# Decode attention with an MLP: the w4 contraction ahead of the last values, outputs laid out by one masked product, the last chunks in two column halves

## The chip, the core and the metric

The kernel runs on one core of a Trainium2 chip. The core has a matrix engine (PE, with a separate row for its weight loads, PEld), a vector engine (DVE), a scalar engine (ACT), a general engine (POOL), a queue that issues most transfers (SP), and 16 DMA engines. Matrix products are written to PSUM, everything else lives in SBUF, and the inputs and the output are in HBM. Each engine works through its own instructions in order; engines wait for each other through semaphores.

The metric is the device time of one execution in microseconds (us), the median over several runs. One more execution is profiled; all durations in this document that are not called a median come from such a profile.

## What is computed

One decode step for 4 sequences, an attention block and an MLP side by side on the same normalized input. The cut reference:

```python
xn = layernorm(x)                                # x: (4, 1, 512)
xa = layernorm(xn)                               # the MLP's own norm; xn is what both blocks get
q  = (xn @ wq).reshape(4, 1, 32, 128).transpose(0, 2, 1, 3)
s  = einsum("bhqd,bhkd->bhqk", q, k_cache) * 128 ** -0.5
o  = einsum("bhqk,bhkd->bhqd", softmax(s), v_cache)
A  = o.transpose(0, 2, 1, 3).reshape(4, 1, 4096) @ wo
B  = xn + gelu(xa @ w3) @ w4                     # with one position, the token mixing adds nothing
out = x + A + B
```

The caches are 4 x 32 x 4096 x 128 in float32: 268 MB each for K and V. wq is 512 x 4096 and wo 4096 x 512 (8.39 MB each), w3 512 x 1792 and w4 1792 x 512 (3.67 MB each). The token mixing shifts along the sequence, which has one position, so all of its shifted parts are zero and w1 and w2 are not read. Everything is float32.

## The kernel before

**Pairs.** The 128 heads (4 sequences of 32) are taken as 64 pairs. K and V of one pair are 4.19 MB each and fill one buffer of 128 partitions x 8192 numbers; partitions 0 to 63 hold the one head, 64 to 127 the other. All large loads, w3, wq (two), K and V, w4 and wo (two), take turns in six such buffers (`slot`, L72), in the order in which the code asks for them; a load is issued by SP when the buffer that is six requests older has been read.

**One pair.** DVE multiplies K by the broadcast query in two pieces (`products`, L199) and adds up along the head dimension (`row_sums`, L203). The maximum over the positions needs a small transpose on PE (`max_begin`, L208 and L210) and a broadcast back (`weights`, L216 to L220). ACT then takes the exponentials (L228) into the blocks of a weight tile that POOL clears (L224). `values` (L238) multiplies weights and V on PE, 16 products of 32 weight columns by 512 columns; product g goes to the partitions 32t to 32t+31 of PSUM with t = g mod 4, which is one of four column groups of the array. In float32 the hardware runs each such product as two passes, so the profile counts twice as many matmuls.

**The loop** (L292 to L313) runs over i from 0 to 64. It asks for K and V of pair i+1, starts pair i on DVE and finishes pair i-1 on ACT and PE. After four pairs `outputs` (L243 to L256) takes the eight heads' results out of PSUM: a copy by ACT into `os`, four products with `sel` and one with `ones` into `oz`, a reciprocal and a product on DVE into `OT`, which has a column for each head. After the 32 heads of a sequence, `spread` (L258 to L264) lays the columns of `OT` out into `lt` with four copies on ACT, each of 32 partitions to every fourth column; the rest of `lt` is zero. One product with `sel` then gives 128 x 32, which becomes `X[:, :, b]`, the left operand for wo.

**The MLP.** `mlp_up` (L269 to L285) runs near the start and leaves gelu(xa @ w3), transposed, in `gT`.

**The end** (L316 to L361). w4 is requested after V of the last pair, wo after w4 in five pieces (chunks 0-15, 16-23, 24-27, 28-30 and 31; a chunk is 128 rows of wo). The first four left operands of w4 are 32 columns wide, zero but for 4, and are made by POOL in the free part of w4's buffer (L321, L322). On PE: `y` gets 14 products with w4 (L341) and those with chunks 0 to 23 (L344), 512 columns each, in four strips of 32 partitions whose sum is wanted. ACT copies `y` to SBUF. `total`, 128 x 128 in PSUM, holds the output's 512 columns as four strips of 128; it was given x + xn at the start (L168). It now gets chunks 24 to 27 (L350), the four strips of `y` added up by a product with `sel` (L352), and chunks 28 to 31 (L355), each as four products of 128 columns. DVE copies `total` to SBUF (L358), and four stores, two each issued by SP and ACT, write the output (L361).

The tile framework orders the instructions of an engine by its own planning and not strictly by the code: on PE one w4 product of `y` stands before `oz`, eight between `oz` and `xt`, and five behind `xt`.

Of the kernel before, what the change touches and what calls it, by code (L numbers as in the profile page):

```python
# [29 lines left out]
F32 = mybir.dt.float32  # L30
AF = mybir.ActivationFunctionType
ALU = mybir.AluOpType
AX = mybir.AxisListType
PSUM = bass.MemoryType.PSUM

P = 128
# [7 lines left out]
def decode_block(ctx: ExitStack, tc: tile.TileContext, x, k, v, wq, wo, w3, w4, out):  # L44
    nc = tc.nc
    B, H, S, DH = k.shape
    D = wq.shape[0]
    F = w3.shape[1]
    NC = D // P
    NF = F // P  # L50
# [3 lines left out]
    NP = B * H // 2  # L54
# [6 lines left out]
    consts = ctx.enter_context(tc.tile_pool(name="consts", bufs=1))  # L61
    kv = ctx.enter_context(tc.tile_pool(name="kv", bufs=SLOTS))
    work = ctx.enter_context(tc.tile_pool(name="work", bufs=2))
    psum = ctx.enter_context(tc.tile_pool(name="psum", bufs=2, space=PSUM))
# [7 lines left out]
    def slot(name):  # L72
        return kv.tile([P, R * DH], F32, tag="kv", name=name)

    def pair_rows(flat, i):
        n = 2 * S * DH
        return flat[i * n:(i + 1) * n].rearrange("(p c d) -> p c d", p=P, c=R)
# [8 lines left out]
    for h in range(2):  # L86
        t = slot(f"wq{h}").rearrange("p (c n) -> p c n", c=NC // 2)
# [5 lines left out]
    def load_k(i):  # L93
        K[i] = slot(f"k{i}").rearrange("p (c d) -> p c d", c=R)
        nc.sync.dma_start(K[i], pair_rows(kf, i))

    def load_v(i):
        V[i] = slot(f"v{i}").rearrange("p (c d) -> p c d", c=R)
        nc.sync.dma_start(V[i], pair_rows(vf, i))
# [6 lines left out]
    ident = consts.tile([P, P], F32, name="ident")  # L106
# [6 lines left out]
    sel = consts.tile([P, 32], F32, name="sel")  # L113
    nc.vector.reduce_sum(sel, ident.rearrange("p (q m) -> p m q", q=4), axis=AX.X)

    selb = consts.tile([P, B, 2, HALF], F32, name="selb")
    for e in range(2):
        a, z = (ident[:, 32 * q:32 * q + B].unsqueeze(2).to_broadcast([P, B, HALF]) for q in (e, e + 2))
# [9 lines left out]
    lt = consts.tile([P, H, 4], F32, name="lt")  # L128

    X = consts.tile([P, WC, B], F32, name="X")  # L130
# [31 lines left out]
    x1nT = lt.rearrange("p h q -> p (h q)").rearrange("p (c m) -> p c m", c=NC)  # L162
    transposed(x1n, x1nT, "x1nT")

    total = psum.tile([P, P], F32, tag="base", bufs=1, name="total")
    for t in range(4):
        for n, src in enumerate((xs, xn)):
            nc.tensor.matmul(total[32 * t:32 * t + 32, :], ident[:B, 0:32], src[:, P * t:P * t + P],  # L168
                             start=(n == 0), stop=False)
    nc.gpsimd.memset(pw_all, 0.0)  # L170
    PW = [pw_all[:, n, :].rearrange("p (g m) -> p g m", g=NG) for n in range(2)]

# [1 line left out]
    q_sb = consts.tile([P, 2, 512], F32, name="q_sb")  # L174
    pq = [psum.tile([P, 512], F32, tag="pv", name=f"pq{n}") for n in range(2)]
    for c in range(NC):
        w = wq_sb[c // 2][:, c % 2, :].rearrange("p (u n j e d) -> p u n e j d", u=2, n=2, j=4, e=2)
        for n in range(2):
            for u in range(2):
                for e in range(2):  # L180
                    r0 = 32 * (2 * u + e)
                    nc.tensor.matmul(pq[n][r0:r0 + 32, :], xnT[:, c, :], w[:, u, n, e],  # L182
                                     start=(c == 0), stop=(c == NC - 1))
# [6 lines left out]
    def queries(z):  # L190
        b, zz = divmod(z, QB)
        u, n = divmod(zz, 2)
        QBC[z] = psum.tile([P, QUAD, DH], F32, tag="qb", name=f"qb{z}")
        nc.tensor.matmul(QBC[z], selb[HALF * u:HALF * (u + 1), b], q_sb[HALF * u:HALF * (u + 1), n, :],  # L194
                         start=True, stop=True)

    def products(i, c0, c1):
        q = QBC[i // QUAD][:, i % QUAD, :].unsqueeze(1).to_broadcast([P, c1 - c0, DH])
        nc.vector.tensor_tensor(out=K[i][:, c0:c1, :], in0=K[i][:, c0:c1, :], in1=q, op=ALU.mult)  # L199

    def row_sums(i):
        sc = work.tile([P, R], F32, tag="sc", name=f"sc{i}")
        nc.vector.reduce_sum(sc, K[i], axis=AX.X)  # L203
        SC[i] = sc

    def max_begin(i):
        rm = work.tile([P, 1], F32, tag="rm", name=f"rm{i}")
        nc.vector.reduce_max(rm, SC[i], axis=AX.X)  # L208
        pm = psum.tile([1, P], F32, tag="b", name=f"pm{i}")
        nc.tensor.matmul(pm, rm, ident, start=True, stop=True)  # L210
        ROWMAX[i] = pm
# [19 lines left out]
    def values(i):  # L231
        z, r = divmod(i, QUAD)
        if r == 0:
            PVS[z] = psum.tile([P, 4 * DH], F32, tag="pv", name=f"pv{z}")
        pw, pv = PW[i % 2], PVS[z]
        for g in range(NG):
            t = g % 4
            nc.tensor.matmul(pv[32 * t:32 * t + 32, :], pw[:, g, :], V[i][:, 4 * g:4 * g + 4, :],  # L238
                             start=(r == 0 and g < 4), stop=(r == QUAD - 1 and g >= NG - 4))

    OT = {}
# [14 lines left out]
        nc.vector.tensor_mul(OT[b][:, 8 * zz:8 * zz + 8], oz[:, 0, :], rz)  # L256

    def spread(b):  # L258
        for q in range(4):
            s = slice(32 * q, 32 * q + 32)  # L260
            nc.scalar.copy(lt[s, :, q], OT[b][s, :])  # L261
        pt = psum.tile([P, 32], F32, tag="b", name=f"xt{b}")
        nc.tensor.matmul(pt, lt, sel, start=True, stop=True)  # L263
        nc.scalar.copy(X[:, :, b], pt)  # L264


    gT = consts.tile([P, NF, B], F32, name="gT")

    def mlp_up():  # L269
        ph = psum.tile([P, FT], F32, tag="qb", name="ph")  # L270
        for c in range(NC):
            for t in range(4):
                nc.tensor.matmul(ph[32 * t:32 * t + 32, :], x1nT[:, c, :],
                                 w3_sb[:, c // 2, c % 2, t * FT:(t + 1) * FT],
                                 start=(c == 0), stop=(c == NC - 1))
        hs, u, t, gt = (w3_slot[:, n * FT:(n + 1) * FT] for n in range(4))
        nc.scalar.copy(hs.rearrange("p (m i) -> p m i", i=32), ph.rearrange("p (i m) -> p m i", i=32))
        nc.vector.tensor_mul(u, hs, hs)
        nc.vector.tensor_scalar(u, u, GELU_B, 1.0, op0=ALU.mult, op1=ALU.add)
        nc.vector.tensor_mul(u, u, hs)  # L280
        nc.scalar.activation(t, u, AF.Tanh, scale=GELU_A)
        nc.vector.tensor_scalar(t, t, 1.0, 0.5, op0=ALU.add, op1=ALU.mult)
        nc.vector.tensor_mul(hs, hs, t)
        nc.vector.transpose(gt, hs)
        nc.vector.tensor_copy(gT, gt.rearrange("p (m i) -> p m i", i=32)[:, :, 0:B])  # L285


    load_v(0)
    queries(0)
    mlp_up()  # L290
    nc.gpsimd.memset(lt, 0.0)
    for i in range(NP + 1):  # L292
        if i + 1 < NP:
            load_k(i + 1)
            load_v(i + 1)
        if i < NP:
            if i % QUAD == 0 and i // QUAD + 1 < NQ:
                queries(i // QUAD + 1)
            products(i, 0, 16)
        if i > 0:  # L300
            weights(i - 1)
        if i < NP:
            products(i, 16, R)
            row_sums(i)
        if i > 0:
            values(i - 1)
            if i % QUAD == 0:
                z = i // QUAD - 1
                outputs(z)
                if z % QB == QB - 1:  # L310
                    spread(z // QB)
        if i < NP:
            max_begin(i)  # L313


    w4_slot = slot("w4")  # L316
    w4_sb = w4_slot[:, :NF * D].rearrange("p (m n) -> p m n", m=NF)
    w4_r = w4.rearrange("(p m) n -> p m n", m=NF)
    nc.sync.dma_start(w4_sb, w4_r)
    gT0 = w4_slot[:, NF * D:NF * D + 4 * 32].rearrange("p (m i) -> p m i", m=4)  # L320
    nc.gpsimd.memset(gT0, 0.0)  # L321
    nc.gpsimd.tensor_copy(gT0[:, :, 0:B], gT[:, 0:4, :])  # L322
    wo_r = wo.rearrange("(p c) n -> p c n", c=WC)
    wo_sb = [slot(f"wo{n}").rearrange("p (c n) -> p c n", c=WC // 2) for n in range(2)]

# [5 lines left out]
    for c0, c1 in ((0, 16), (16, CUT), (CUT, 28), (28, 31), (31, WC)):  # L331
        wo_load(c0, c1)

    def wo_part(c, c0=0, c1=D):
        return wo_sb[c // 16][:, c % 16, c0:c1]


    y = psum.tile([P, D], F32, tag="qb", name="y")
    for m in range(NF):
        t, g, rows = (m, gT0[:, m, :], 32) if m < 4 else (m % 4, gT[:, m, :], B)  # L340
        nc.tensor.matmul(y[32 * t:32 * t + rows, :], g, w4_sb[:, m, :], start=(m < 4), stop=False)  # L341
    for c in range(CUT):
        t = (c + 2) % 4
        nc.tensor.matmul(y[32 * t:32 * t + B, :], X[:, c, :], wo_part(c), start=False, stop=(c >= CUT - 4))  # L344

    ys = os.rearrange("p m d -> p (m d)")
    nc.scalar.copy(ys, y)
    for c in range(CUT, 28):
        for t in range(4):
            nc.tensor.matmul(total[32 * t:32 * t + B, :], X[:, c, :], wo_part(c, P * t, P * t + P), start=False, stop=False)  # L350
    for t in range(4):
        nc.tensor.matmul(total[32 * t:32 * t + 32, :], sel, ys[:, P * t:P * t + P], start=False, stop=False)  # L352
    for c in range(28, WC):
        for t in range(4):
            nc.tensor.matmul(total[32 * t:32 * t + B, :], X[:, c, :], wo_part(c, P * t, P * t + P),  # L355
                             start=False, stop=(c == WC - 1))
    r = q_sb[:, 0, 0:P]
    nc.vector.tensor_copy(r, total)  # L358
    for t in range(4):
        queue = nc.sync if t % 2 == 0 else nc.scalar  # L360
        queue.dma_start(out.rearrange("b s d -> (b s) d")[:, P * t:P * t + P], r[32 * t:32 * t + B, :])  # L361


# [26 lines left out]
```

## Time and profile before

| | |
|---|---|
| median of 3 runs | 1314.33 us (1314.22 to 1314.59) |
| profiled execution | 1314.51 us |
| its span, first to last instruction | 1312.7 us |
| read from HBM | 561.00 MB |
| DVE busy | 1160.6 us |
| PE busy | 522.3 us |
| mean granted clock of PE | 0.644 |
| last product of `total` ends, copy begins | 1309.71 us |

The span lies 1.8 us under the execution's time, which also holds what comes before the first and after the last instruction. A line of the profile's chain gives a start, a duration and what ran or was waited for. A line of a source view gives an instruction, its count, the least, median and greatest duration in ns, and the first and last start. A window line gives start and end, the length, then for PE, PEld, DVE, ACT and POOL the busy time and number of instructions, and at the end the granted PE clock as a share of full speed, the busy share of the DMA engines and GB/s. Matmul durations include their passage through the array; what counts in a stream is the distance between starts.

### The profile page before, as it was taken

How to read it: one execution, taken by the hardware profiler on the slowest of the kernel's cores; microseconds unless marked ns; L12 is line 12 of the kernel's file. 1: busy time of each engine (PE TensorE's matmuls, PEld its weight loads, DVE VectorE, ACT ScalarE, POOL GpSimd, SP SyncE). 2: the span in 40 equal slices, each digit the busy share in tenths (PEclk: the TensorE clock that was granted, in tenths of full speed). 3: DMA queues.
4: the chain of work that ended last, by engine and by line, in shares of the span. 5: the costliest groups of instructions: out<-in, count | busy, mean ns of one | idle time of the engine just before them, and what ended most of it. 6: DMA issues, size and time to landing. Idle time of an engine off the chain costs nothing.

```text
span 1312.7 us, 7037 instructions
## 1 busy us (share of the span) xinstructions
PE 522.3 (40%) x2780; PEld 170.0 (13%) x2780; DVE 1160.6 (88%) x381; ACT 86.5 (7%) x365; POOL 15.7 (1%) x78
## 2 busy tenths in 40 slices
PE   4424335334424424434434433443342442442346
PEld 2101101111111101111111110111111110110112
DVE  2798999999999999989989999999998989999992
ACT  0100000000000000000010000000000000000001
POOL 0000000000000000000000000000000000000000
PEclk9566576666666566656666766656666656656757
DMA  9999999999999999999999999999999999999997
GB/s 402 429 434 431 431 433 430 431 430 433 431 431 430 432 431 432 430 431 432 431 432 432 432 431 431 431 431 430 431 431 431 432 431 431 431 430 432 432 430 317
DMA packets 19944, 561.46 MB, mean 428 GB/s; under 512 B 2228, under 2 KB 2244, under 8 KB 2504
## 3 DMA queue, kind: packets, MB, share of 16 engines
q1 hardware_dynamic: 19888, 561.00, 99.4%
q8 instruction: 22, 0.36, 0.1%
q14 instruction: 10, 0.08, 0.0%
q10 hardware_dynamic: 24, 0.01, 0.0%
HBM read 561.00 MB, written 0.01 MB: 427 GB/s over the span
## 4 chain that ended last, share of the span: by engine, by line
DMA 52%; DVE 36%; PE 8%; issue 2%; ACT 1%; SPq 0%; DVEq 0%
DMA k<-in_A_k_cache_dram 52%; DVE sc L203 20%; DVE k L199 15%; PE pv L238 5%; PE oz L248 1%; PE pm L210 1%; PE pn L218 0%; ACT os L245 0%; PE y L344 0%; DVE gm L216 0%; PE y L341 0%; DVE rm L208 0%; PE oz L251 0%; ACT lt L261 0%; PE xt L263 0%
## 5 line engine op out<-in xcount | busy, mean ns | idle before, releaser
L199 DVE TENSOR_TENSOR k<-k,qb 128x2048 f32<-128x2048 f32 (+1 forms) x128 | 559.9, 4415 | 56.9 <-DMA k<-in_A_k_cache_dram 56.6
L203 DVE TENSOR_REDUCE sc<-k 128x64 f32<-128x8192 f32 x64 | 555.5, 8679 | 5.1 <-DVE rz L253 0.2
L238 PE MATMUL pv<-v,pw 128*32 128x512 f32 x2048 | 373.1, 895 | 81.0 <-issue 81.0
L210 PE MATMUL pm<-ident,rm 128*1 128x128 f32 x128 | 37.4, 395 | 591.7 <-DVE rm L208 591.7
L238 PEld LDWEIGHTS pv<-v,pw 128*32 128x32 f32 x2048 | 93.3, 156 | 305.4 <-issue 305.4
L210 PEld LDWEIGHTS pm<-ident,rm 128*1 128x1 f32 x128 | 7.2, 80 | 637.8 <-issue 628.0
L220 ACT COPY nm<-pn 128x2 f32<-128x2 f32 x64 | 10.3, 161 | 1024.6 <-PE pn L218 1024.6
L216 DVE TENSOR_REDUCE gm<-pm 1x2 f32<-1x128 f32 x64 | 17.8, 278 | 52.4 <-PE pm L210 52.4
L218 PE MATMUL pn<-gm,ones 1*128 1x2 f32 x128 | 37.2, 358 | 24.2 <-DVE gm L216 24.2
L228 ACT ACTIVATE pw<-sc,nm 64x64 f32<-64x64 f32 x128 | 44.6, 348 | 6.0
L218 PEld LDWEIGHTS pn<-gm,ones 1*128 1x128 f32 x128 | 31.8, 306 | 56.1 <-DVE gm L216 53.3
L194 PE MATMUL qb<-q_sb,selb 64*128 64x512 f32 x32 | 19.9, 703 | 25.2 <-DVE k L199 24.6
L224 POOL MEMSET pw<- 128x128 f32 x64 | 13.1, 205 | 1199.1 <-PE pv L238 1199.0
L228 ACT ACTIVATION_READ_ACCUMULATOR pw<-sc,nm 64x1 f32 x128 | 23.7, 185 | 0.0
L248 PE MATMUL oz<-sel,os 128*128 128x8 f32 x128 | 16.9, 259 | 10.5 <-ACT os L245 10.5
L248 PEld LDWEIGHTS oz<-sel,os 128*128 128x128 f32 x128 | 15.5, 191 | 25.6 <-ACT os L245 25.6
L253 DVE RECIPROCAL rz<-oz 128x8 f32<-128x8 f32 x16 | 3.3, 206 | 15.7 <-PE oz L251 15.6
L245 ACT COPY os<-pv 128x512 f32<-128x512 f32 x16 | 9.4, 586 | 95.4 <-PE pv L238 95.4
L208 DVE TENSOR_REDUCE rm<-sc 128x1 f32<-128x64 f32 x64 | 14.1, 220 | 1.7
L263 PE MATMUL xt<-sel,lt 128*128 128x32 f32 x8 | 2.3, 380 | 29.9 <-ACT lt L261 29.9
L182 PE MATMUL pq<-wq,X 128*32 128x512 f32 x64 | 10.6, 820 | 8.7 <-DMA wq<-in_A_wq_dram 8.7
L194 PEld LDWEIGHTS qb<-q_sb,selb 64*128 64x128 f32 x32 | 5.1, 200 | 40.7 <-DVE k L199 37.7
(77 smaller groups left out, 79.5 us busy)
## 6 DMA issues: line engine op xcount, KB each, us to landing
k<-in_A_k_cache_dram SPq DMA_DIRECT2D x64, 4096.0 KB, 40.7
v<-in_A_v_cache_dram SPq DMA_DIRECT2D x64, 4096.0 KB, 41.3
wq<-in_A_wq_dram SPq DMA_DIRECT2D x2, 4096.0 KB, 16.9
wo<-in_A_wo_dram SPq DMA_DIRECT2D x1, 4096.0 KB
w<-in_B_w_dram SPq DMA_DIRECT2D x2, 1792.0 KB, 7.6
w<-in_B_w_dram SPq DMA_DIRECT2D x1, 3584.0 KB
wo<-in_A_wo_dram SPq DMA_DIRECT2D x1, 2048.0 KB, 34.7
wo<-in_A_wo_dram SPq DMA_DIRECT2D x1, 1024.0 KB
```

What stands on the lines that cost most here:

```text
L182: nc.tensor.matmul(pq[n][r0:r0 + 32, :], xnT[:, c, :], w[:, u, n, e], start=(c == 0), stop=(c == NC - 1))
L194: nc.tensor.matmul(QBC[z], selb[HALF * u:HALF * (u + 1), b], q_sb[HALF * u:HALF * (u + 1), n, :], start=True, stop=True)
L199: nc.vector.tensor_tensor(out=K[i][:, c0:c1, :], in0=K[i][:, c0:c1, :], in1=q, op=ALU.mult)
L203: nc.vector.reduce_sum(sc, K[i], axis=AX.X)
L208: nc.vector.reduce_max(rm, SC[i], axis=AX.X)
L210: nc.tensor.matmul(pm, rm, ident, start=True, stop=True)
L216: nc.vector.tensor_reduce(gm, ROWMAX[i].rearrange("o (e p) -> o e p", e=2), axis=AX.X, op=ALU.max, negate=True)
L218: nc.tensor.matmul(pn, ones[0:1, :], gm, start=True, stop=True)
L224: nc.gpsimd.memset(pw[:, :, 8 * r2:8 * r2 + 8], 0.0)
L228: nc.scalar.activation(o, sc[s, :].rearrange("p (g w) -> p g w", w=4), AF.Exp, bias=nm[s, e:e + 1], scale=1.0, accum_out=rs[s, r, e:e + 1])
L238: nc.tensor.matmul(pv[32 * t:32 * t + 32, :], pw[:, g, :], V[i][:, 4 * g:4 * g + 4, :], start=(r == 0 and g < 4), stop=(r == QUAD - 1 and ...
L248: nc.tensor.matmul(oz[:, 0, :], os[:, m, :], sel.rearrange("p (r m e) -> p m r e", m=4, e=2)[:, m], start=(m == 0), stop=(m == 3))
```

## The change

- w4 is requested, and its left operands are made, ahead of V of the last pair (`w4_load`), and its 14 products are issued ahead of the last `values` (`mlp_down`).
- `spread` lays `OT` out with one DVE product, `OT` broadcast along 4 columns times a mask that is 1 where the column is the partition's quarter. The mask is one reduction of the identity at the start. Clearing `lt` before the loop goes away, since the product writes all of it.
- `total` is 64 x 256, two strips of 256 columns. Each product into it, at the start and for chunks 24 to 31 and `sel`, is two products of 256 columns instead of four of 128; the last copy is 64 x 256, and there are two stores.

```diff
--- before.py
+++ after.py
@@ -113,6 +113,9 @@
     sel = consts.tile([P, 32], F32, name="sel")
     nc.vector.reduce_sum(sel, ident.rearrange("p (q m) -> p m q", q=4), axis=AX.X)
 
+    mask = consts.tile([P, 4], F32, name="mask")
+    nc.vector.reduce_sum(mask, ident.rearrange("p (q m) -> p q m", q=4), axis=AX.X)
+
     selb = consts.tile([P, B, 2, HALF], F32, name="selb")
     for e in range(2):
         a, z = (ident[:, 32 * q:32 * q + B].unsqueeze(2).to_broadcast([P, B, HALF]) for q in (e, e + 2))
@@ -162,11 +165,14 @@
     x1nT = lt.rearrange("p h q -> p (h q)").rearrange("p (c m) -> p c m", c=NC)
     transposed(x1n, x1nT, "x1nT")
 
-    total = psum.tile([P, P], F32, tag="base", bufs=1, name="total")
-    for t in range(4):
+    total = psum.tile([2 * 32, D // 2], F32, tag="base", bufs=1, name="total")
+
+    def part(t):
+        return slice(t * (D // 2), (t + 1) * (D // 2))
+
+    for t in range(2):
         for n, src in enumerate((xs, xn)):
-            nc.tensor.matmul(total[32 * t:32 * t + 32, :], ident[:B, 0:32], src[:, P * t:P * t + P],
-                             start=(n == 0), stop=False)
+            nc.tensor.matmul(total[32 * t:32 * t + 32, :], ident[:B, 0:32], src[:, part(t)], start=(n == 0), stop=False)
     nc.gpsimd.memset(pw_all, 0.0)
     PW = [pw_all[:, n, :].rearrange("p (g m) -> p g m", g=NG) for n in range(2)]
 
@@ -256,9 +262,7 @@
         nc.vector.tensor_mul(OT[b][:, 8 * zz:8 * zz + 8], oz[:, 0, :], rz)
 
     def spread(b):
-        for q in range(4):
-            s = slice(32 * q, 32 * q + 32)
-            nc.scalar.copy(lt[s, :, q], OT[b][s, :])
+        nc.vector.tensor_mul(lt, OT[b].unsqueeze(2).to_broadcast([P, H, 4]), mask.unsqueeze(1).to_broadcast([P, H, 4]))
         pt = psum.tile([P, 32], F32, tag="b", name=f"xt{b}")
         nc.tensor.matmul(pt, lt, sel, start=True, stop=True)
         nc.scalar.copy(X[:, :, b], pt)
@@ -284,14 +288,33 @@
         nc.vector.transpose(gt, hs)
         nc.vector.tensor_copy(gT, gt.rearrange("p (m i) -> p m i", i=32)[:, :, 0:B])
 
+    w4_r = w4.rearrange("(p m) n -> p m n", m=NF)
+    W4 = {}
+
+    def w4_load():
+        t = slot("w4")
+        W4["w"] = t[:, :NF * D].rearrange("p (m n) -> p m n", m=NF)
+        nc.sync.dma_start(W4["w"], w4_r)
+        W4["g"] = t[:, NF * D:NF * D + 4 * 32].rearrange("p (m i) -> p m i", m=4)
+        nc.gpsimd.memset(W4["g"], 0.0)
+        nc.gpsimd.tensor_copy(W4["g"][:, :, 0:B], gT[:, 0:4, :])
+
+    def mlp_down():
+
+        W4["y"] = psum.tile([P, D], F32, tag="qb", name="y")
+        for m in range(NF):
+            t, g, rows = (m, W4["g"][:, m, :], 32) if m < 4 else (m % 4, gT[:, m, :], B)
+            nc.tensor.matmul(W4["y"][32 * t:32 * t + rows, :], g, W4["w"][:, m, :], start=(m < 4), stop=False)
+
 
     load_v(0)
     queries(0)
     mlp_up()
-    nc.gpsimd.memset(lt, 0.0)
     for i in range(NP + 1):
         if i + 1 < NP:
             load_k(i + 1)
+            if i + 1 == NP - 1:
+                w4_load()
             load_v(i + 1)
         if i < NP:
             if i % QUAD == 0 and i // QUAD + 1 < NQ:
@@ -302,6 +325,8 @@
         if i < NP:
             products(i, 16, R)
             row_sums(i)
+        if i == NP:
+            mlp_down()
         if i > 0:
             values(i - 1)
             if i % QUAD == 0:
@@ -313,13 +338,6 @@
             max_begin(i)
 
 
-    w4_slot = slot("w4")
-    w4_sb = w4_slot[:, :NF * D].rearrange("p (m n) -> p m n", m=NF)
-    w4_r = w4.rearrange("(p m) n -> p m n", m=NF)
-    nc.sync.dma_start(w4_sb, w4_r)
-    gT0 = w4_slot[:, NF * D:NF * D + 4 * 32].rearrange("p (m i) -> p m i", m=4)
-    nc.gpsimd.memset(gT0, 0.0)
-    nc.gpsimd.tensor_copy(gT0[:, :, 0:B], gT[:, 0:4, :])
     wo_r = wo.rearrange("(p c) n -> p c n", c=WC)
     wo_sb = [slot(f"wo{n}").rearrange("p (c n) -> p c n", c=WC // 2) for n in range(2)]
 
@@ -331,14 +349,10 @@
     for c0, c1 in ((0, 16), (16, CUT), (CUT, 28), (28, 31), (31, WC)):
         wo_load(c0, c1)
 
-    def wo_part(c, c0=0, c1=D):
-        return wo_sb[c // 16][:, c % 16, c0:c1]
-
-
-    y = psum.tile([P, D], F32, tag="qb", name="y")
-    for m in range(NF):
-        t, g, rows = (m, gT0[:, m, :], 32) if m < 4 else (m % 4, gT[:, m, :], B)
-        nc.tensor.matmul(y[32 * t:32 * t + rows, :], g, w4_sb[:, m, :], start=(m < 4), stop=False)
+    def wo_part(c):
+        return wo_sb[c // 16][:, c % 16, :]
+
+    y = W4["y"]
     for c in range(CUT):
         t = (c + 2) % 4
         nc.tensor.matmul(y[32 * t:32 * t + B, :], X[:, c, :], wo_part(c), start=False, stop=(c >= CUT - 4))
@@ -346,19 +360,18 @@
     ys = os.rearrange("p m d -> p (m d)")
     nc.scalar.copy(ys, y)
     for c in range(CUT, 28):
-        for t in range(4):
-            nc.tensor.matmul(total[32 * t:32 * t + B, :], X[:, c, :], wo_part(c, P * t, P * t + P), start=False, stop=False)
-    for t in range(4):
-        nc.tensor.matmul(total[32 * t:32 * t + 32, :], sel, ys[:, P * t:P * t + P], start=False, stop=False)
+        for t in range(2):
+            nc.tensor.matmul(total[32 * t:32 * t + B, :], X[:, c, :], wo_part(c)[:, part(t)], start=False, stop=False)
+    for t in range(2):
+        nc.tensor.matmul(total[32 * t:32 * t + 32, :], sel, ys[:, part(t)], start=False, stop=False)
     for c in range(28, WC):
-        for t in range(4):
-            nc.tensor.matmul(total[32 * t:32 * t + B, :], X[:, c, :], wo_part(c, P * t, P * t + P),
+        for t in range(2):
+            nc.tensor.matmul(total[32 * t:32 * t + B, :], X[:, c, :], wo_part(c)[:, part(t)],
                              start=False, stop=(c == WC - 1))
-    r = q_sb[:, 0, 0:P]
+    r = q_sb[:2 * 32, 0, 0:D // 2]
     nc.vector.tensor_copy(r, total)
-    for t in range(4):
-        queue = nc.sync if t % 2 == 0 else nc.scalar
-        queue.dma_start(out.rearrange("b s d -> (b s) d")[:, P * t:P * t + P], r[32 * t:32 * t + B, :])
+    for t, queue in enumerate((nc.sync, nc.scalar)):
+        queue.dma_start(out.rearrange("b s d -> (b s) d")[:, part(t)], r[32 * t:32 * t + B, :])
 
 
 # ---- launch: one core; inputs and outputs as the reference has them ----
```

In the changed kernel's own numbering L199, L203, L210 and L238 become L205, L209, L216 and L244; the w4 products become L307, the lay-out product is L265 and its matmul L267, the wo products L358, the products into `total` L364, L366 and L369, the last copy L372 and the stores L374.

## The prediction

> **What bounds the kernel now.** First the page's engine shares and its 40 slices.
>
> ```profile
> PE 522.3 (40%) x2780; PEld 170.0 (13%) x2780; DVE 1160.6 (88%) x381; ACT 86.5 (7%) x365; POOL 15.7 (1%) x78
> ...
> DMA  9999999999999999999999999999999999999997
> ```
>
> The DMA engines are full in every slice but the last, so a pair of heads costs what its 8.39 MB cost at 431 GB/s, 19.4 us. DVE is busy 88%, and still waits for K (56.6 us over 64 pairs). Only what comes after the last loads can be shortened. Next, the chain of waits in its last stretch (start us, us, what).
>
> ```profile
> 1270.35 8.76 DVE k L199 x2
> ...
> 1291.09 5.32 PE pv L238 x32
> 1296.41 0.83 PE y L341 x2
> 1297.25 0.99 PE oz L248 x8
> 1298.24 0.22 PE oz L251 x2
> 1298.46 1.85 PE y L341 x13
> 1300.31 0.34 PE xt L263 x2
> 1300.65 1.38 PE y L341 x9
> ...
> 1302.46 4.41 PE y L344 x44
> 1306.87 0.34 PE total L350 x7
> ...
> 1308.77 0.92 PE total L355 x32
> 1309.68 0.02 issue
> 1309.71 0.29 DVE q_sb L358
> ```
>
> From the last K (1270.3) the chain is DVE's, from 1291.1 PE's, and the w4 contraction (L341) stands between the last values and wo. Last, the wo loads (L328: first and last issue, time to landing) and the DMA share in two of the last microseconds (the DMA share and GB/s are the two last columns).
>
> ```profile
> L328 SPq DMA_DIRECT2D wo<-in_A_wo_dram x5: 327/427/430, 1258.3 to 1269.8; - x5
> ...
> DMA to landing us min/median/max: 34.7/38.2/38.3
> ```
>
> ```profile
> 1303.00:1304.00 1.00, 1.00 (x12) 0.21 (x8) 0.00 (x0) 0.00 (x0) 0.00 (x0) 1.00 0.68 281
> ...
> 1307.00:1308.00 1.00, 1.00 (x25) 0.58 (x23) 0.00 (x0) 0.30 (x1) 0.00 (x0) 1.00 0.09 35
> ```
>
> The first wo load is issued at 1258.3; the other four stand 0.43 us apart from 1268.5 (where row sums of pair 62 free their buffer) to 1269.8. So chunks 16-23 land at 1268.5+34.7 = 1303.2, 28-30 at 1269.4+38.2 = 1307.6, 31 at 1308.1. Bytes behind K63 fit: 14.15 MB (v63, w4, 24 chunks) by 1303.2 and 16.25 MB by 1308.1 are both 430 GB/s. On that line, chunks 0-15 land at 1298.4 and 24-27 at 1305.7 (estimates). PE reaches each later (24-27 at 1306.6, 28-30 at 1308.6): today PE sets the end, but the loads lie only 1 us under it, and that is the most any shortening of PE's tail is worth.
>
> **The change, part by part.**
>
> *w4 ahead of v63.* The order of transfers becomes K63, w4, v63, wo; bytes and buffer waits stay, each issue taking its neighbour's wait (w4 goes out when values 60 end, 1238.3; v63 when row sums 61 end, 1249.1; wo as before). No queue runs dry, since a K takes 40.7 us from issue to landing, four transfers deep. So w4 lands at 1270.3 + 3.67 MB/430 = 1278.8, v63 at 1288.6, where the values need it at 1291.1: 2.5 us of cover. The POOL work in w4's buffer (two instructions of 0.20 us) stands behind the last clearing of the weights (1258.4), long before 1278.8; nothing follows it there.
>
> *The contraction moves.* In the changed kernel's instruction order the 28 matmul passes stand on PE between values(62), which end at 1278.2, and the last row-maximum transpose (L210, ready at 1288.2). Four passes on four column groups leave every 0.43 us in the tail (L344's weight loads are 0.43 us apart), or 0.107 us each, 0.21 at half clock: 3 to 6 us, done by 1284.8 at the latest. Cover: PE's 10.13 us idle before L210. If w4 came after 1282.2, L210 and all behind it (maximum, exponentials, values) would wait, one for one.
>
> *Outputs laid out by one product.* Four ACT copies (L261) are 1.02 us; a DVE product of 128x128 is not in the trace. Between 128x8 (0.168) and 128x2048 (2.28), on the straight line 0.29. In three earlier pairs it takes 0.29 of DVE, covered by its 0.58 us wait for K and less than the ACT copies that PE waited for there. The mask (one reduction; L114's, larger, is 0.35) and the regrouped first matmuls lie in the first 14 us, where the first PE work that needs a load starts at 18.1. Without that cover 0.35.
>
> *Start of the wo chunks.* Values end 1296.4, os copy and oz to 1298.46, reciprocal and product to 1298.91, all as now; then 0.29 for lt, 0.41 for xt, 0.22 for X, and some 0.2 of hand-overs: first wo pass at 1300.05. Now its stream of 48 passes (5.12 us) effectively runs 1302.3 to 1307.45, since L341's rest is ahead of it. Gain 2.25: the stream ends at 1305.2.
>
> *Two column halves.* Now 72 passes of 128 columns (L350, L352, L355) go to four column groups: 0.107 us each by L344's rate, four at a time, 1.92 us (L355: 32 passes started within 0.87). After, 36 passes of 256 columns take 0.213 each, but `total` has two strips, so two run at a time: 36 x 0.213/2 = 3.84. Columns stay, groups halve: +1.92. Bounds: 1.92 if the array gave two groups the rate of four, 3.84 if not. L194 on the whole array (two passes of 512 columns span 1.12 us with 0.69 of the last one's own) gives one per 0.43 us, while L344 gets four of them; so concurrency comes from the groups and I take 3.84.
>
> *Sum for PE.* L364 waits for chunks 24-27 (1305.7), so 0.5 of the 2.25 is given to the load: 1305.7 + 3.84 + 0.17 (last matmul's drain: L344's 0.592 less 0.427) = 1309.7, against 1309.68 now. Chunks 28-31 (1307.6, 1308.1) come before their turn at 1307.85. Zero.
>
> *Copy and stores.* 64x256 from PSUM instead of 128x128 (0.292): at the 1.04 ns per column of the line above +0.13 (bounds 0 and +0.29). Stores: two of 2 KB on each queue, the second issued 0.33 us after the first; now one each, -0.33 (bounds -0.35 and 0).
>
> Sum: 0 + 0.13 - 0.33 = -0.2. The profiled execution has a span of 1312.7 in 1314.51, 1.8 around it, and lies 0.18 above the median of 1314.33; from the median, 1314.1.
>
> **The clock.** The granted clock is 0.5 until PE has worked through a stretch, then 1.0. It falls in stretches of 3.41 us: it rose at 1256.99 and fell at 1260.40 with PE busy 1.22 us of these (36%), and rose at 1236.50 and stayed past 1239.91 with 1.76 (52%). Without L341 PE idles about 0.7 us before oz, 0.8 before xt and 0.3 before wo; laid on the same stretches (edge at 1297.94) it works 66% of the next: kept. Another phase may give near 50%, which is a rival. The Trainium skill, TensorE: Matmul & The Clock Gate, "What's actually happening", has the clock fall after an idle window of some 3.4 us. By that rule no gap here is long enough and the rival has no price; the 36% row speaks against it, so I keep the rival.
>
> **The rivals.**
>
> 1. *Balance, forecast:* what the early contraction frees, loads and the halved groups take back. 1314.1, own range 1313.7 to 1314.6.
>
> 2. *Two groups at the rate of four.* Then only the loads bind: chunk 31 lands at 1308.1, plus 0.2 for its passes, 0.17 and hand-over: 1308.6, 1.1 earlier than now; with -0.2, 1313.0. For: the columns streamed are the same. Against: L194.
>
> 3. *The clock falls in the idle tail.* 3.41 us of the wo stream at half rate is 1.7 us lost; it ends at 1306.9, the halves start 1.2 later than in the forecast: 1315.3. For: the 36% row. Against: the 66%.
>
> 4. *The wait for w4 takes over the end, slower.* y stands in front of L210 on PE. If w4 and v63 shared the engines instead of following each other, w4 would land with v63 near 1288.6, and L210 would start at 1291.6 to 1294.6 instead of 1288.3: 3.3 to 6.3 later, less the 0.5 that the load took, 1317 to 1320. It decides from a landing at 1282.2. For: issues are up to 11 us apart and several transfers are outstanding. Against: V lands one transfer time behind its K and the wo landings fit one line, as in a queue served in order.
>
> 5. *The head start is simply not used:* the tail as now and +1.9 for the halves; needs an xt late by 2 us, for which no row speaks: 1316.
>
> **Chances.** Forecast 0.67, two groups at full rate 0.10, clock 0.14, w4 wait 0.05, no head start 0.04. A measurement tells about 0.2% (2.6 us) from no change. Only rival 4 reaches +2.6 surely; the last K and the wo loads forbid -2.6, short of loads that end earlier (0.04). Faster 0.04, same 0.90, slower 0.06. The range reaches to rivals 2 and 3: 1313.0 to 1315.5.
>
> **What would show it.** L307 starting near 1278.8 and over before L216 (the old L210); L358's first pass near 1300; L364 starting when a load lands, not when y ends; 36 passes of L364 to L369 in 3.8 us; the end of PE near 1309.7 and one store per queue. Wrong: L216 waiting on PE, a granted clock of 0.5 behind 1298, wo landing elsewhere than at 1303 to 1308, or L364 to L369 in 2 us.

## The result, and the profile after

The changed kernel takes 1317.11 us (median of 22 runs, 1314.51 to 1318.47), the kernel before 1314.09 (22 runs, 1313.28 to 1315.56): ratio 1.0019, 95% interval 1.0013 to 1.0026. It is slower by 0.2%, and it is uneven: of its 22 times 9 lie between 1314.5 and 1315.6, 13 between 1316.7 and 1318.5. The forecast was 1314.1 with a range up to 1315.5, so the shorter group lies inside it or 0.1 above and the longer one well outside. The profiled execution, 1314.51 us with a span of 1312.6, is of the shorter group.

That profile alone would have confirmed the forecast. Its last stretch in the chain of waits (start us, us, what):

```profile
1267.64 37.95 DMA wo<-in_A_wo_dram
1305.59 0.04 issue
1305.63 1.90 PE total L364 x16
1307.53 0.43 PE total L366 x4
1307.96 1.75 PE total L369 x16
1309.71 0.02 issue
1309.73 0.42 DVE q_sb L372
```

Where the kernel before had a row of PE work from 1291 on, the chain goes through a load of wo: PE waits until 1305.6 for chunks 24 to 27 and then needs 4.08 us for the halves and their drain. The moved contraction, in the timeline (start, us, engine, line, operation; in brackets the idle time before it and its releaser):

```profile
1277.73 1.06 PE L307 MATMUL y<-w 128*32 128x512 f32 x8 [2.21 <-DMA w<-in_B_w_dram]
...
1278.59 2.77 PE L307 MATMUL y<-w,gT 128*4 128x512 f32 x20
...
1287.06 0.59 PE L216 MATMUL pm<-ident,rm 128*1 128x128 f32 x2 [5.70 <-DVE rm L214]
```

It starts when w4 lands and is over 5.7 us before PE is needed again. Nothing here is slow. What the longer executions do can only be read from a profile of one of them.

### The profile page after: what moved, and what is told of

Read it like the earlier page. It is cut to its first block, busy times and chain, and to the rows that moved or that the text cites. A ratio compares the mean times of both kernels' runs of the same rounds, so it can differ in the third digit from the quotient of the medians.

```text
span 1312.6 us, 6935 instructions
## 1 busy us (share of the span) xinstructions
PE 522.8 (40%) x2736; PEld 169.0 (13%) x2736; DVE 1161.9 (89%) x386; ACT 82.6 (6%) x349; POOL 15.4 (1%) x77
## 4 chain that ended last, share of the span: by engine, by line
DMA 58%; DVE 33%; PE 6%; issue 2%; ACT 0%; SPq 0%; DVEq 0%
DMA k<-in_A_k_cache_dram 55%; DVE sc L209 19%; DVE k L205 13%; PE pv L244 4%; DMA wo<-in_A_wo_dram 3%; PE oz L254 1%; PE pm L216 0%; ACT os L251 0%; PE pn L224 0%; DVE gm L222 0%; DVE rm L214 0%; PE oz L257 0%; PE total L364 0%; PE total L369 0%; SPq L88 0%
## 5 line engine op out<-in xcount | busy, mean ns | idle before, releaser
L205 DVE TENSOR_TENSOR k<-k,qb 128x2048 f32<-128x2048 f32 (+1 forms) x128 | 560.0, 4415 | 58.1 <-DMA k<-in_A_k_cache_dram 57.9
L209 DVE TENSOR_REDUCE sc<-k 128x64 f32<-128x8192 f32 x64 | 555.5, 8679 | 4.9
L244 PE MATMUL pv<-v,pw 128*32 128x512 f32 x2048 | 371.2, 891 | 81.0 <-issue 79.8
L216 PE MATMUL pm<-ident,rm 128*1 128x128 f32 x128 | 37.4, 395 | 590.0 <-DVE rm L214 590.0
L244 PEld LDWEIGHTS pv<-v,pw 128*32 128x32 f32 x2048 | 92.9, 156 | 304.0 <-issue 302.7
L216 PEld LDWEIGHTS pm<-ident,rm 128*1 128x1 f32 x128 | 7.1, 80 | 635.8 <-issue 626.5
L214 DVE TENSOR_REDUCE rm<-sc 128x1 f32<-128x64 f32 x64 | 14.1, 220 | 1.7
L267 PE MATMUL xt<-sel,lt 128*128 128x32 f32 x8 | 2.2, 365 | 29.3 <-DVE lt L265 29.3
L372 DVE COPY q_sb<-total 64x256 f32<-64x256 f32 x1 | 0.4, 416 | 11.5 <-PE total L369 11.5
```

## The experiments

Two theories stood against each other. *Clock:* without the w4 products PE stands idle in its tail, the granted clock falls there in some executions, and the wo stream runs at half rate. *Loads:* the wo loads land late in some executions, and the halves behind them hand the lateness on.

### The changed kernel again

The changed kernel ran three more times without an edit: e1 with 11 timed executions, of which one was profiled, and e5 and e6 with one profiled execution each.

> The changed kernel once more, for a profile of one of its long executions (22 of them lay in two groups, 1314.5 to 1315.6 and 1316.7 to 1318.5, the profiled one in the first). Clock theory: PE stands idle in its tail without the w4 products, its granted clock falls there in some executions, and the wo stream runs at half rate for 3.4 to 6.8 us; a long execution shows a clock of 0.5 somewhere between the end of the last values and the end of y, and weight loads of the wo stream 0.85 us apart. Load theory: the clock stays at 1.0, the wo loads land late in some executions, and the halves behind them (3.84 us) hand the lateness on, where the kernel before had 1 us of cover; a long execution shows the first product for chunks 24 to 27 starting more than 36.5 us after the third wo issue. Both: median near 1317, 2.5 to 3.5 above the kernel before.

> The changed kernel, one look, for a profile of a long execution (18 of its 33 executions so far took over 1316 us). Clock theory: if the time is over 1316, the clock is 0.5 for two windows of 3.41 us in the wo stream, y ends after 1307, and the first product for chunks 24 to 27 follows y; if it is under 1316, the clock is 1.0 there or falls for one window at most. Load theory: if the time is over 1316, the clock is 1.0 and the product waits for its load.

> The same look once more, with the same expectations as e5_look.

e1: median 1315.42 (1314.49 to 1318.09; ratio 1.0013, 1.0004 to 1.0022), 5 of 11 over 1316. A median near 1317 was expected; with two groups 3 us apart the median depends on how many executions fall into the longer one, 13 of 22 the first time and 5 of 11 here. e5 took 1317.77 and e6 1314.53. Over all 35 times of the changed kernel, 19 are over 1316; the median of the shorter 16 is 1314.7, of the longer 19 it is 1317.8.

e5, of 1317.77, is a profile of a long execution. Its chain of waits:

```profile
1297.92 1.06 PE oz L254 x8
...
1300.12 0.62 PE xt L267 x2
...
1301.03 7.98 PE y L358 x48
1309.02 1.73 PE total L364 x16
1310.74 0.43 PE total L366 x4
1311.17 1.75 PE total L369 x16
```

There is no load in it any more. The 48 passes of y take 7.98 us instead of the 5.33 that they take at full clock in e6, and L364 follows y. Up to the last values the two are alike: the last row maximum (L214) starts at 1287.92 in e5 and at 1287.88 in e6. Its loads had landed long before:

```profile
L346 SPq DMA_DIRECT2D wo<-in_A_wo_dram x5: 327/426/430, 1257.4 to 1269.8; - x5
...
DMA to landing us min/median/max: 34.7/38.2/40.9
```

The least and the median are those of the kernel before, 34.7 and 38.2: chunks 28 to 30, issued near 1269.4, are there near 1307.6, 3.5 us before their turn at 1311.2. The load theory falls for this execution. The same profile in windows of 3.41 us, cut at the edges of its clock (after the length: busy time and number of instructions of PE, PEld, DVE, ACT, POOL, then the granted clock, the DMA share, GB/s):

```profile
1296.17:1299.59 3.42, 2.32 (x22) 1.32 (x14) 0.31 (x2) 0.59 (x1) 0.00 (x0) 1.00 0.97 411
1299.59:1303.00 3.41, 2.58 (x14) 0.91 (x18) 0.35 (x2) 0.22 (x1) 0.00 (x0) 0.50 0.90 375
1303.00:1306.41 3.41, 3.41 (x20) 0.59 (x16) 0.00 (x0) 0.00 (x0) 0.00 (x0) 0.50 0.48 196
1306.41:1309.82 3.41, 3.41 (x34) 0.93 (x28) 0.00 (x0) 0.59 (x1) 0.00 (x0) 1.00 0.07 26
```

The clock column is the finding: granted at 1296.17, taken back at 1299.59, given again at 1306.41. Two windows of the tail are cold, which here means a granted clock of 0.5. The first cold window is not full of work, since y begins at 1301.03, and does not bring the clock back; the second is, and does.

e1's own profile (1314.66) shows a fall that costs nothing. Its clock falls at 1299.76 for one window, y takes 7.03 us from 1298.56, and ends when chunks 24 to 27 land. It has room for this because its last K, like that of the first profile, came 1.2 us earlier than in e5 and e6 (1269.1 against 1270.3). It also shows what the clock goes by. PE's busy time in the window in which the clock could fall, first the profile of 1314.51 in which it stayed, then that of e1 in which it was taken back at the end of the window (busy time and instructions, clock, DMA share, GB/s):

```profile
1297.31:1300.73 3.42, 2.20 (x20) 1.00 0.99 415
```

```profile
1296.35:1299.76 3.41, 2.19 (x20) 1.00 0.99 417
```

Equal. The same windows, counting only the products into y, which stream 512 columns each:

```profile
1297.31:1300.73 3.42, 1.68 (x16) 1.00 0.99 415
```

```profile
1296.35:1299.76 3.41, 1.21 (x12) 1.00 0.99 417
```

The rest is oz and xt, products of 8 and 32 columns, which keep PE busy by the profile's count and did not hold the clock. One pair is two windows. All windows of the five profiles (the kernel before, the changed kernel four times) that begin with a granted clock and hold PE work, but none other than V, y, oz and xt products, say the same: the clock stayed at the end of 158 of them, with 1.38 us or more of V and y products, and fell at the end of 170, with 1.39 us or less. By PE's busy time they cannot be told apart: in the kernel before, the window from 437.79 has PE busy for 2.60 us, 1.32 of it V products, and lost the clock, while the one from 1236.50 in the prediction, busy for only 1.76 us, all of it V products, kept it.

### PE kept busy

Two products that nothing reads, in the two gaps.

```diff
+        if z == NQ - 1:                                   # behind oz
+            junk = psum.tile([P, 384], F32, tag="pv", name="junk")
+            nc.tensor.matmul(junk, ident, os.rearrange("p m d -> p (m d)")[:, 0:384], start=True, stop=True)
...
+        if b == B - 1:                                    # behind xt
+            junk = psum.tile([P, P], F32, tag="pv", name="junk2")
+            nc.tensor.matmul(junk, ident, lt.rearrange("p h q -> p (h q)"), start=True, stop=True)
```

> The changed kernel with two products on PE whose results nothing reads, one of 384 columns between oz and xt and one of 128 columns between xt and wo, 0.9 us of work in gaps of 0.85 and 0.3 us. Clock theory: PE stays busy, the clock does not fall, the longer group is gone, median 1314.3 to 1315.3. Load theory: nothing changes, median 1316.5 to 1317.5 in two groups.

Median 1314.51 (1314.28 to 1316.93; ratio 1.0004, 0.9995 to 1.0013); one of 11 over 1316. More work made the kernel shorter, which of the two theories only the clock theory allows. The one long execution was not profiled. In the profile that there is the clock stays at 1.00, but its two windows from 1294.84 hold 1.63 us of V and 1.59 us of y products beside the unread ones, so the clock would by the boundary above have stayed without them; the evidence here is the count. A profile whose windows fall as badly as those of e5, with the same unread products, follows below in e11.

Next, the same gaps filled with products of 8 columns.

```diff
+            junk = psum.tile([P, 2 * QUAD], F32, tag="pv", name="junk")
+            for m in range(3):
+                nc.tensor.matmul(junk, os[:, m, :], sel[:, 0:8], start=(m == 0), stop=(m == 2))
...
+            junk = psum.tile([P, 2 * QUAD], F32, tag="pv", name="junk2")
+            nc.tensor.matmul(junk, lt, sel[:, 0:8], start=True, stop=True)
```

> The changed kernel with unread products as in e2_fill, in the same two gaps and of about the same length on PE, but of 8 columns each (three between oz and xt, one between xt and wo), so that PE loads weights and streams almost nothing. If the clock follows PE's busy time: as e2_fill, median 1314.3 to 1315, at most 2 of 11 above 1316. If it follows the columns streamed: as the changed kernel, 4 or more of 11 above 1316, median 1315.4 to 1317.5.

Median 1315.19 (1313.95 to 1317.88; ratio 1.0011, 1.0003 to 1.0020), 4 of 11 over 1316, three of these over 1317.6. The count is the one expected if columns decide, the median lies 0.2 under the range; 4 of 11 against 1 of 11 and 19 of 35 is a lean and no proof. What carries the point are the windows above.

### The parts alone

Of the change, the early w4 alone, put into the kernel before; its load and its contraction behind the loop are taken out.

```diff
+            if i + 1 == NP - 1:
+                w4_load()
             load_v(i + 1)
...
+        if i == NP:
+            mlp_down()
         if i > 0:
             values(i - 1)
```

> The kernel before with w4 loaded and contracted early and nothing else: four ACT copies, four strips, four stores. Clock theory: PE's gap before xt is 0.7 us longer than in the changed kernel, so the clock falls at least as often as there; executions without a fall end by the loads at 1313.0 to 1313.5, with one cold window near 1313.5 to 1314.5, with two near 1315 to 1316.5; median 1314.5 to 1316, spread over 2.5 us. Load theory: four strips cover the loads, one group at 1313 to 1314.

The four copies, strips and stores are left as they were. 1315.86 (1313.60 to 1316.74; ratio 1.0009, 1.0000 to 1.0018): five times from 1313.6 to 1314.2, six from 1315.9 to 1316.7. Two groups appear with this part alone; the best time is 0.4 above the least of the kernel before beside it (1313.17). That best execution is the profiled one, and it too has a cold window, from 1300.11 to 1303.52, with y taking 7.03 us; none of the six longer ones was profiled.

The masked lay-out alone, in the kernel before:

```diff
-        for q in range(4):
-            s = slice(32 * q, 32 * q + 32)
-            nc.scalar.copy(lt[s, :, q], OT[b][s, :])
+        nc.vector.tensor_mul(lt, OT[b].unsqueeze(2).to_broadcast([P, H, 4]), mask.unsqueeze(1).to_broadcast([P, H, 4]))
```

> The kernel before with the masked product on DVE alone. PE works through its w4 products while ACT copies, so 0.73 us less before xt moves w4 products from before xt to behind it and ends nothing earlier: within 0.3 us of the kernel before in either theory. A gain of 0.7 would say that PE's tail has waited for the copies.

1314.61 (1313.93 to 1315.20; ratio 1.0003, 0.9994 to 1.0011): no gain and no loss that can be told. In its chain xt starts 0.98 us after the end of `oz`, against 1.85 in the kernel before, and y's w4 products stand behind it instead.

The two halves and two stores alone, in the kernel before:

```diff
-    total = psum.tile([P, P], F32, tag="base", bufs=1, name="total")
+    total = psum.tile([2 * 32, D // 2], F32, tag="base", bufs=1, name="total")
...
-        for t in range(4):
-            nc.tensor.matmul(total[32 * t:32 * t + B, :], X[:, c, :], wo_part(c, P * t, P * t + P), start=False, stop=False)
+        for t in range(2):
+            nc.tensor.matmul(total[32 * t:32 * t + B, :], X[:, c, :], wo_part(c, HF * t, HF * t + HF), start=False, stop=False)
```

> The kernel before with total in two halves and two stores alone. PE's tail works without a gap here. Both theories: 1.9 for the groups, 0.13 for the copy, less 0.33 for the stores: 1.7 above the kernel before, 1315.8. Clock theory: a spread as narrow as that of the kernel before (about 1.5 us). Load theory: the same, since PE reaches every load after its landing. A spread of 4 us in two groups here would say that the halves alone make the long group.

1316.89 (1314.91 to 1317.71; ratio 1.0018, 1.0009 to 1.0026), ten of 11 between 1316.3 and 1317.7. On its own this part costs about as much as the whole change, and without two groups; in its profile PE has no gap in the tail and the clock stays at 1.00 from 1294.6 on. The median lies 2.6 above the kernel before beside it (1314.29), where 1.7 was expected. The profile (1316.47, span 1314.6) shows 1.9 of this: the end of PE at 1311.53, 1.85 after that of the kernel before, which is the groups, and 0.13 for the copy. The other term, the stores, was hardly there: from the first store's issue to the end of the span it takes 2.6 us with two stores and 2.7 with four. The remaining 0.7 of the median stays open.

The change without its halves:

```diff
-    total = psum.tile([2 * 32, D // 2], F32, tag="base", bufs=1, name="total")
+    total = psum.tile([P, P], F32, tag="base", bufs=1, name="total")
...
-        return slice(t * (D // 2), (t + 1) * (D // 2))
+        return slice(t * P, (t + 1) * P)
...
-        for t in range(2):
+        for t in range(4):
...
-    for t, queue in enumerate((nc.sync, nc.scalar)):
+    for t, queue in enumerate((nc.sync, nc.scalar, nc.sync, nc.scalar)):
```

> The changed kernel with total in four strips of 128 columns and four stores as before; w4 early and the lay-out product stay. Both theories: the end is 1.9 us shorter by the groups, 0.33 longer by the stores, 0.13 shorter by the copy. Clock theory: two groups of times 2 to 3 us apart remain, the shorter near 1313.0, the longer near 1315.5. Load theory: one group, median 1313.5 to 1314.5, since lateness up to 1 us is covered again.

1314.96 (1313.23 to 1316.52; ratio 1.0004, 0.9995 to 1.0013): four times from 1313.2 to 1313.5, seven from 1314.9 to 1316.5. The groups remain and both lie lower. In its profile (1314.88) the clock is 0.5 from 1298.61 to 1305.44 and y takes 7.99 us.

### A version under both

The changed kernel with the two unread products of 384 and 128 columns, four strips and four stores; one kernel, measured twice.

> The changed kernel with the two unread products of e2_fill and with the four strips and stores of e3_strips. Clock theory: no fall, PE waits for the loads only: chunk 31 lands near 1307.7, its products, copy and stores follow, 1313.1 to 1313.5 with a narrow spread, about 1 us under the kernel before. Load theory: as e3_strips, since the clock has no part, near 1315 with a spread of 3 us.

> e8_fill_strips once more, to see whether it lies under the kernel before: 1313.2 to 1313.5 against 1314.0 to 1314.3, ratio 0.9993, nearly all of its executions within 0.4 us of each other.

e8: 1313.28 (1313.13 to 1314.86; ratio 0.9994, 0.9985 to 1.0003), ten of 11 under 1313.5. e11: 1313.04 (1312.96 to 1313.12; ratio 0.9990, 0.9981 to 0.9999). The second interval lies under 1, the first just not; the kernel before had 1314.06 and 1314.20 beside them. All 11 times of e11 are within 0.16 us, and its median is 0.2 under the range that was expected. The 1314.86 of e8 was not profiled. In e11's profile the windows fall as badly as in e5: the clock rises at 1295.72, late in the last values. The window that begins there, with the V products alone and then with the unread product alone:

```profile
1295.72:1299.13 3.41, 1.08 (x12) 1.00 0.98 417
```

```profile
1295.72:1299.13 3.41, 0.47 (x2) 1.00 0.98 417
```

In e5, with 1.04 us of V products in that window, the clock fell; here 1.55 us of wide products stand in it, and the clock stays to 1312.79. This is the most direct evidence that the unread products hold the clock. The end of e11, in the timeline:

```profile
1305.56 1.06 PE L370 MATMUL total<-wo,X 128*4 128x128 f32 x32
...
1307.17 1.06 PE L375 MATMUL total<-wo,X 128*4 128x128 f32 x32 [0.25 <-DMA wo<-in_A_wo_dram]
1308.30 0.29 DVE L378 COPY q_sb<-total 128x128 f32<-128x128 f32 x1 [8.72 <-PE total L375]
```

PE is done with everything before the last chunks land, and the span ends 4.2 us after their landing. This is what the early contraction is worth once PE keeps its clock and uses all four groups: 0.8 (e8) and 1.2 us (e11), about the distance to the loads that the prediction read from the kernel before.

## Why the prediction was wrong

**Its sum was right for the execution it described.** Forecast for the span 1312.5, profiled 1312.6. w4's products start at 1277.7 (forecast 1278.8, and the last K came 1.2 earlier in that execution than in the profile before) and end 5.7 us before L216. The lay-out product takes 0.29 (0.29). Chunks 24 to 27 release L364 at 1305.6 (1305.7). The halves and their drain take 4.08 (4.01). PE ends at 1309.71 (1309.7), and the copy takes 0.42 (0.42). The stores' term failed: -0.33 was forecast for one issue less on each queue, and issue to end takes 2.46 to 2.6 us with two stores against 2.6 to 2.7 with four, some 0.1. What hides the second issue was not followed.

**The step that failed is "The clock", and with it rival 3.** Three things in it:

- *One phase taken for all.* It laid the tail on the edges of the one profile it had (1297.94, "it works 66% of the next: kept"). The clock rises during the last values at 1294.54 in the kernel before's profile and at 1293.90, 1292.93, 1296.17 and 1295.27 in the four of the changed kernel (the first, e1, e5, e6). The worst phase is one in which the clock rises late in the last values: it then has only their rest, 1.0 us in e5, and oz in its first window. In e6, 0.9 us earlier, it has 1.46 us of them and stays.
- *Busy time taken for work.* The 66% counted oz and xt. Of 2.20 and 2.19 us of equally busy windows one kept the clock and one lost it; the wide products, 1.68 and 1.21, tell them apart.
- *One cold window priced, where there are two.* The price was 1.7 us of stream less 0.5, a time of 1315.3, with a chance of 0.14. In the long execution e5 y loses 2.65 us against e6 (7.98 less 5.33), since the first cold window begins with PE idle and does not bring the clock back. The late rise also makes the values 6.17 us instead of 5.74, and xt, in the cold window, takes 0.61 instead of 0.38. Together these are the 3.3 us by which L364 starts later, 1309.0 instead of 1305.7, and the span is 1316.0 instead of 1312.7. Of the 35 executions 19 were of the long group; this is the only one of them with a profile, so that the others lost the same two windows is inferred from their times. e3's profile, with four strips, shows the same two windows and 7.99 us.

So the forecast's direction came from the wrong case. The early contraction did take 3 us of work out of PE's tail, and that work had been what kept the clock: in the kernel before PE is busy in all of 1294.54 to 1301.36.

The Trainium skill, TensorE: Matmul & The Clock Gate, "What's actually happening", calls the window free-running, which the moving edges here agree with, and has the clock fall after an idle window. By that rule no execution would have lost it, as no gap of PE reaches 1 us in the tails of the four profiles: 1314.1. Here, in e5, it fell after a window with PE busy 68% of the time, so the measurement decides against that sentence.

**The other rivals.** Two groups at the rate of four (2) is refuted by e4: +1.85 at PE's end. The wait for w4 (4) did not occur: 2.2 us of idle PE before L307, 5.7 after. The unused head start (5), at 1316, comes nearest to the longer group's 1317.8, but with the wrong cause: xt started 0.5 us later in e5 than in e6 and not 2, and y itself was slow.

**The load floor held.** 1 us was called the most that PE's tail can give; the version that waits for the loads alone gained 0.78 (e8, 1314.06 to 1313.28) and 1.16 (e11, 1314.20 to 1313.04).

**The halves** were priced rightly and cover for them was counted rightly in the short group, where they cost 1.0 to 1.4 (e2 lies 0.22 above the kernel before beside it, e8 and e11 0.78 and 1.16 under it). They are the other half of the result: without them, even with the falling clock, the change is within noise of the kernel before (e3).

## What to carry to other kernels

Work that is moved away from between two bursts of PE also takes away what kept its clock granted: before moving it, ask how many us of wide products remain in each window of 3.41 us, for every position of the window (here it took about 1.4), and price two cold windows and not one. A single profile of a kernel whose end depends on such a phase is one draw; look at the scatter of the times first, and take profiles until one of each group is there. Small left operands should spread over all four column groups: here 16 passes of 256 columns on two groups took 1.90 us (L364), 32 passes of 128 columns on four took 1.06 (e11's L370).

## What the runs showed of the hardware

The granted clock goes by wide products and not by PE's busy time: windows of 3.41 us with PE busy 2.2 to 2.3 us lost it when only 1.0 to 1.2 of these were products of 512 columns, and kept it with 1.7; over all windows of the 13 profiles that hold only V, y, oz and xt products the boundary lies between 1.33 and 1.40 us, whatever the busy time (2.61 lost it, 1.41 kept it). It came back after a window that PE had filled for 2.66 of 3.41 us (before, up to 1216.04), and not after one with 2.40 (up to 1274.07); in such windows of the 13 profiles the boundary lies at 2.6. Two narrow strips halve PE's rate: 256-column passes on two groups and 128-column passes on four gave an end 1.85 us apart over 36 and 72 passes. And halving the number of small stores saved some 0.1 us of the 0.33 that an issue takes.
